# Chunk attention and a feed-forward layer on one core: V of the first two tiles by parity halves into one home, w_in's first half by pairs of K slices, and another order of the first loads and of the second tile's attention

## The chip, the cores and the metric

The kernel runs on one core of a Trainium2 chip. The metric is the device time of one execution in microseconds (us). TensorE is called PE, its weight load PEld, VectorE DVE, ScalarE ACT, GpSimd POOL, and SyncE, whose queue issues all DMAs here, SP.

## The reference

```python
# q, k, v: [8 batches, 8 heads, 576, 64], float32; chunks of 64 tokens
scores = q_c @ k_c.T / sqrt(64)            # within each chunk of 64 x 64
attn = softmax(scores); out = attn @ v_c
x = out.transpose(0, 2, 1, 3).reshape(4608, 512)
h = x @ w_in                               # 512 x 2048
g = 0.5 * h * (1 + erf(h / sqrt(2)))       # exact gelu
return g @ w_out                           # 2048 x 512, float32
```

## The kernel before

The 4608 tokens are cut into nine tiles of 512: tile t from 0 to 7 holds the first 512 tokens of batch t, and tile 8 the last chunk of every batch. For each tile the kernel computes attention, whose result `x` is kept transposed (model dimension on the partitions, four K slices of 128), then h = gelu(x @ w_in) in sixteen slots f of 128 hidden columns, then y = h @ w_out. All matmul operands are bf16; the inputs arrive as float32 in a pool of six 1 MB stage tiles (`arrival`) and are cast by DVE, ACT or POOL. Tile 0 multiplies densely; from tile 1 on seven products replace eight in both matrix products.

Everything is in program order on each engine (a manual schedule): where an instruction stands in the code sets when its engine gets to it. The attention of tiles 0 and 1 is cut into units per group g of two heads (G = 4): `T[2g]` and `T[2g+1]` transpose Q and K on PE (L207) and copy the results out of PSUM (Q by ACT at L213, K by ACT or DVE into the block-diagonal `k_bd` at L220), `S_[g]` is the scores (L366) and their exp on ACT (`pT`, L368), `att_sum` and `att_sums` the sums for the softmax (L374, L392), with reciprocals and transposes on DVE and `rb` copies on ACT (L403), and `A[g]` the product with V (L440) and its scaling into `x` on DVE (L442). The transposes of tile 1 share two PSUM banks (`ps_tp`), scores and outputs three (`ps_at`), h and y of tile 0 three (`ps_mm`).

V sits in `v_bd`, a block-diagonal home: head 2g fills rows 0 to 63 and columns 0 to 63 of a 128x128 block, head 2g+1 the other corner, and the other corners are zeros that a memset writes once. Tile 0 and tile 1 have a home each. V's loads bring 128 tokens on 128 partitions, so two chunks, and each head takes two casts (`cast_v`, L201), one for each chunk parity.

The order of tile 1's units between tile 0's y matmuls is written out as a table of hooks in `phase(0, {...})`: the number is a step of the second product. Steps 0 to 11 are slots f of h for all four row blocks (`mm2_rows`, L1025, four y matmuls each), steps 12 to 15 finish one row block each (`mm2_slot`, L989, four y matmuls). In slots 2 to 4 and in all of tile 0's h, `by_halves` (L465) splits each 512-column matmul in two. After the row blocks `rows_out` (L1004) copies y to `y_sb`, by ACT for the first three and by DVE for the last; the stores (L999), the DMA transposes of tile 2's Q and K (`flip`, L229) and V's rows (L152) follow on SP. Tile 1's h (L481, L491) comes next on PE, and tile 2's scores (L264) and V product (L349) within it and the second product of tile 1.

The loads at the start go out on SP in this order: Q and K of tile 0, V by head (L181), w_in in seven pieces (L1067), then w_out in four parts of 1 MB (L1075) with Q and K of tile 1 between them (L142), and V of tile 1.

Of the kernel before, what the change touches and what calls it, by code (L numbers as in the profile page):

```python
# [11 lines left out]
def kernel(  # L12
# [54 lines left out]
    NV = 2  # L67
    v_bds = [consts.tile([P, CT, G, P], bf16, name=f"v_bd{i}") for i in range(NV)]
    k_bds = [consts.tile([P, CT, P], bf16, name=f"k_bd{i}") for i in range(G)]

    def zero_v(i, eng):
        eng.memset(v_bds[i][0:CH, :, :, CH:P], 0.0)
        eng.memset(v_bds[i][CH:P, :, :, 0:CH], 0.0)

    def zero_k(k_bd, eng):
        eng.memset(k_bd[0:CH, :, CH:P], 0.0)
        eng.memset(k_bd[CH:P, :, 0:CH], 0.0)
# [120 lines left out]
    def cast_v(t, g, r, copies):  # L198
        to = slice(CH * r, CH * (r + 1))
        for c, copy in enumerate(copies):  # L200
            copy(v_bds[t % NV][to, c:CT:2, g, to], tiles[t]["vf"][CH * c:CH * (c + 1), 2 * g + r])  # L201

# [232 lines left out]
    def att_av(t, g):  # L435
        st = tiles[t]
        pool, tag = (ps_tp, "tp") if t == 1 and g > 1 else (ps_at, "at")
        av_ps = pool.tile([P, CT, CH], f32, tag=tag, name="av_ps")
        for i in range(CT):
            nc.tensor.matmul(av_ps[:, i, :], v_bds[t % NV][:, i, g, :], st["pT", g][:, i, :], start=True, stop=True)  # L440
        x, av, rc = st["x"][:, g, :], av_ps[:].rearrange("p i e -> p (i e)"), st["rc", g][:]
        nc.vector.tensor_tensor(x, av, rc.rearrange("p n e -> p (n e)"), op=mybir.AluOpType.mult)  # L442
# [17 lines left out]
    def by_halves(to, left, right, start, stop):  # L460

        n = to.shape[-1] // 2
        for a in range(2):
            cols = slice(n * a, n * (a + 1))
            nc.tensor.matmul(to[:, cols], left, right[:, cols], start=(start and a == 0), stop=stop, skip_group_check=True)  # L465

    def mm1_slices(t, pools, steps):

        st = tiles[t]
        st["h"] = hpool.tile([P, FF, MT], bf16, tag="h", name="h")  # L470
        h_ps = {}
        for step in steps:
            if callable(step):
                step()
                continue
            for ks in step[1]:
                for f in step[0]:
# [3 lines left out]
                    (nc.tensor.matmul if t else by_halves)(h_ps[f][:], w_in_sb[:, ks, f * P:(f + 1) * P], st["x"][:, ks, :],  # L481
                                                           start=(ks == 0), stop=(ks == KS - 1))
                    if ks == KS - 1:
                        nc.scalar.activation(st["h"][:, f, :], h_ps[f][:], Act.Gelu)

    def mm1_slot(t, f):
        if f == 0:
            tiles[t]["h"] = hpool.tile([P, FF, MT], bf16, tag="h", name="h")
        h_ps = ps_mm.tile([P, MT], f32, tag="mm", name="h_ps")
        for ks in range(KS):  # L490
            (nc.tensor.matmul if t else by_halves)(h_ps[:], w_in_sb[:, ks, f * P:(f + 1) * P], tiles[t]["x"][:, ks, :],  # L491
                                                   start=(ks == 0), stop=(ks == KS - 1))
        nc.scalar.activation(tiles[t]["h"][:, f, :], h_ps[:], Act.Gelu)  # L493
# [42 lines left out]
    def t_sum(i):  # L536
        v2 = v_bds[(i - 1) // 2][:].rearrange("p a b c -> p (a b c)")
        n = HF * HD
        return v2[:, (i - 1) % 2 * n:((i - 1) % 2 + 1) * n].rearrange("p (f n) -> p f n", f=HF)
# [472 lines left out]
    def mm2_rows(t, f):  # L1012

        last = MT // P - 1
        if f == 0:
            order = [(last, 0), (0, 0), (1, 0)]
        elif f == 1:
            order = [(last, 1), (0, 1), (1, 1), (2, 0), (2, 1)]
        else:
            order = [(ms, f) for ms in range(MT // P)]  # L1020
        for ms, fi in order:
            if fi == 0:
                pool, tag = (ps_at, "at") if ms == last else (ps_mm, "mm")
                tiles[t]["y_ps", ms] = pool.tile([P, d_model], f32, tag=tag, name="y_ps")
            (by_halves if 2 <= f < 5 else nc.tensor.matmul)(  # L1025
                tiles[t]["y_ps", ms][:], tiles[t]["h"][:, fi, ms * P:(ms + 1) * P], w_out_sb[:, fi, :],
                start=(fi == 0), stop=False)
# [35 lines left out]
    def load_w_in(c, parts=1):  # L1063
        raw = stage_tile()[:].rearrange("p (ks n) -> p ks n", ks=KS)
        n = WC // parts
        for a in range(parts):
            nc.sync.dma_start(raw[:, :, a * n:(a + 1) * n], w_in_v[:, :, c * WC + a * n:c * WC + (a + 1) * n])  # L1067
# [3 lines left out]
        return cast  # L1071
# [25 lines left out]
    with tc.manual_schedule():  # L1097
# [4 lines left out]
        win = [load_w_in(c, 2) for c in range(NWC - 1)]  # L1102
        act_table(Act.Exp)
# [6 lines left out]
        zero_k(k_bds[2], nc.gpsimd)  # L1110
        cast_qk(0, "k", 1, PO)
        zero_k(k_bds[3], nc.gpsimd)
        cast_qk(0, "k", 2, PO)
        cast_qk(0, "k", 3, PO)
        for g in range(G - 1):
            for r in range(2):
                cast_v(0, g, r, (PO, PO))
        cast_v(0, G - 1, 0, (PO, PO))
        win[0](0, PO)
# [29 lines left out]
        cast_v(0, G - 1, 1, (DV, DV))  # L1149
        A[2]()  # L1150
        win[0](1, AC)
        p3()
        A[3]()
        win.append(load_w_in(NWC - 1))
        wout = [load_w_out(0)]
        win[0](2, DV)
        win[0](3, PO)
        load_qk(1, "q")
        wout.append(load_w_out(1))
        for c in range(1, NWC):  # L1160
# [4 lines left out]
            if c == 1:  # L1165
                load_qk(1, "k")
            else:
                wout.append(load_w_out(c))
            if c < 3:
                r = slice(CH * (c - 1), CH * c)  # L1170
                o = slice(CH * (2 - c), CH * (3 - c))
                nc.gpsimd.memset(v_bds[1][r, :, :, o], 0.0)
# [9 lines left out]
        weight_sum(1)  # L1182
        for g in range(G):
            cast_qk(1, "k", g, DV if g % 2 == 0 else PO)
        for i in range(FC):
            wout[2](i, PO)
        for i in range(2):
            wout[3](i, PO)
        for g in (0, 2, 3):
            for r in range(2):  # L1190
                cast_v(1, g, r, (PO, PO))
# [7 lines left out]
        def sums():  # L1199
# [56 lines left out]
        for t in range(1, NT):  # L1256
# [8 lines left out]
            if t == 1:  # L1265
# [4 lines left out]
                for g in range(G):  # L1270
                    cast_qk(2, "k", g, DV)
# [96 lines left out]
```

## Time and profile before

| | us |
|---|---|
| median of 3 runs | 267.25 |
| lowest and highest | 266.49, 268.29 |
| the profiled execution's own time | 267.09 |
| its span in the profile | 265.5 |

| engine | busy us | share of the span |
|---|---|---|
| PE | 256.1 | 96% |
| DVE | 223.1 | 84% |
| ACT | 190.5 | 72% |
| POOL | 103.2 | 39% |

The span runs from the first to the last instruction of the one execution that the profiler recorded. Busy time is the time in which an engine had an instruction under way. A timeline row gives the start, the length, the engine and line, what is written and read, how many instructions it groups, and in brackets the idle time before it and what ended it. The mean granted clock of PE was 0.997.

### The profile page before, as it was taken

What the parts mean: (1) busy time and instruction counts of PE and PEld (TensorE: products, weight loads), DVE (VectorE), ACT (ScalarE), POOL (GpSimd) and SP (SyncE); (2) the same over time, 40 slices, a digit from 0 to 9 for tenths busy, and PEclk for the clock granted to TensorE, in tenths of its full rate; (3) what the DMA queues carried; (4) which work ended last, traced back from release to release, by engine and by line L of the source; (5) the groups of instructions that cost most, each with busy time, mean ns of one, the idle gap of its engine ahead of it and who ended that gap; (6) DMA issues with size and microseconds to landing.
All of it is one profiled execution on the core that took longest, in us unless ns stands there. A gap on an engine that the chain in (4) does not pass through costs nothing.

```text
span 265.5 us, 7854 instructions
## 1 busy us (share of the span) xinstructions
PE 256.1 (96%) x3122; PEld 210.6 (79%) x3122; DVE 223.1 (84%) x394; ACT 190.5 (72%) x386; POOL 103.2 (39%) x225
## 2 busy tenths in 40 slices
PE   6789999999999999999999999999999999999993
PEld 2478875556888888887888888888888888888882
DVE  6874986898897599678999999999999999948772
ACT  3856758987767987898888588947894789227720
POOL 7767778702364291481372095009411300000000
PEclk9999999999999999999999999999999999999998
DMA  6999998999979979999999988998973410130014
GB/s 201 268 311 396 395 401 236 283 193 289 243 195 284 220 175 244 275 239 249 276 245 232 267 186 237 217 175 195 264 160 80 134 42 2 41 119 3 2 40 125
DMA packets 123416, 54.02 MB, mean 203 GB/s; under 512 B 97776, under 2 KB 120304, under 8 KB 123376
## 3 DMA queue, kind: packets, MB, share of 16 engines
q1 hardware_dynamic: 123072, 53.23, 77.4%
q8 instruction: 25, 0.41, 0.7%
q10 hardware_dynamic: 304, 0.26, 0.3%
q14 instruction: 15, 0.12, 0.1%
HBM read 36.70 MB, written 9.44 MB: 174 GB/s over the span
## 4 chain that ended last, share of the span: by engine, by line
PE 76%; DMA 10%; ACT 7%; SPq 4%; issue 1%; DVE 0%; POOL 0%
PE hs_ps L601 31%; PE y_ps L761 22%; PE y_ps L791 13%; DMA arrival<-in_moe_w_out_dram 8%; ACT h L609 3%; SPq L181 2%; PE h_ps L491 2%; DMA arrival<-in_moe_w_in_dram 2%; PE av_ps L349 2%; PE h_ps L481 2%; ACT pT L272 2%; SPq L142 1%; PE y_ps L1025 1%; PE y_ps L989 1%; PE s_ps L264 1%; ACT L1095 1%
## 5 line engine op out<-in xcount | busy, mean ns | idle before, releaser
L609 ACT ACTIVATE h<-hs_ps 128x512 bf16<-128x512 f32 x87 | 49.6, 609 | 6.5 <-PE hs_ps L601 5.7
L238 POOL CAST v_nat<-arrival 128x256 bf16<-128x256 f32 x56 | 24.9, 473 | 33.5 <-DMA arrival<-in_v_dram 23.1
L601 PEld LDWEIGHTS <-w_in_sb 128*128 128x128 bf16 x348 | 33.9, 98 | 4.7 <-issue 0.2
L194 POOL CAST q_nat<-arrival 128x256 bf16<-128x256 f32 x40 | 16.8, 467 | 50.2 <-DMA arrival<-in_k_dram 25.3
L601 PE MATMUL hs_ps<-x,w_in_sb 128*128 128x256 bf16 x232 | 31.8, 272 | 0.0
L761 PEld LDWEIGHTS <-h 128*128 128x128 bf16 x240 | 23.2, 98 | 2.8
L1095 ACT ACT_TABLE_LOAD x16 | 20.5, 1283 | 1.3 <-PEq L1352 1.0
L190 POOL CAST k_nat<-arrival 128x256 bf16<-128x256 f32 (+1 forms) x44 | 19.1, 476 | 5.3 <-DMA arrival<-in_k_dram 5.3
L721 ACT COPY kept<-y_ps 128x512 f32<-128x512 f32 (+1 forms) x17 | 9.0, 536 | 16.0 <-PE y_ps L761 15.9
L761 PE MATMUL y_ps<-w_out_sb,h 128*128 128x256 bf16 x160 | 18.6, 273 | 0.0
L761 PE MATMUL y_ps<-v_bd,k_bd 128*128 128x256 bf16 x160 | 18.5, 273 | 0.1
L761 PEld LDWEIGHTS <-k_bd 128*128 128x128 bf16 x160 | 15.6, 98 | 2.1 <-issue 0.2
L618 ACT COPY hs_ps<-hs_ps 128x512 f32<-128x512 f32 x29 | 16.2, 583 | 0.6 <-PE hs_ps L601 0.5
L601 PE MATMUL hs_ps<-k_bd,w_in_sb 128*128 128x256 bf16 x116 | 16.6, 272 | 0.0
L493 ACT ACTIVATE h<-h_ps 128x512 bf16<-128x512 f32 x21 | 12.5, 604 | 5.5 <-PE h_ps L465 4.1
L272 ACT ACTIVATE pT<-s_ps 128x512 bf16<-128x512 f32 x28 | 14.4, 599 | 1.8 <-PE s_ps L264 1.8
L791 PEld LDWEIGHTS <-h 128*128 128x128 bf16 x144 | 13.8, 98 | 1.7
L465 PE MATMUL h_ps<-x,w_in_sb 128*128 128x256 bf16 x128 | 14.5, 273 | 0.1
L601 PE MATMUL hs_ps<-k_bd,w_in_more 128*128 128x256 bf16 x96 | 14.2, 273 | 0.0
L601 PEld LDWEIGHTS <-w_in_more 128*128 128x128 bf16 x128 | 12.5, 98 | 2.0 <-issue 0.3
L726 DVE TENSOR_TENSOR kept<-y_ps,kept 128x512 f32<-128x512 f32 (+1 forms) x16 | 10.4, 651 | 4.3 <-PE y_ps L761 2.3
L465 PEld LDWEIGHTS <-w_in_sb 128*128 128x128 bf16 x128 | 12.3, 98 | 2.1 <-DVE w_in_sb L1070 0.7
(175 smaller groups left out, 638.9 us busy)
## 6 DMA issues: line engine op xcount, KB each, us to landing
arrival<-in_v_dram SPq DMA_DIRECT2D x58, 128.0 KB, 3.2
arrival<-in_k_dram SPq DMA_DIRECT2D x28, 256.0 KB, 5.6
arrival<-in_q_dram SPq DMA_DIRECT2D x7, 1024.0 KB, 6.9
out_dram<-kept SPq DMA_DIRECT2D x24, 256.0 KB, 3.2
arrival<-in_moe_w_out_dram SPq DMA_DIRECT2D x4, 1024.0 KB, 12.1
arrival<-in_moe_w_in_dram SPq DMA_DIRECT2D x6, 512.0 KB, 8.5
out_dram<-y_sb SPq DMA_DIRECT2D x8, 256.0 KB, 2.5
arrival<-in_v_dram SPq DMA_DIRECT2D x28, 64.0 KB, 2.7
```

The costliest lines, as they stand in the source:

```text
L190: copy(st[nm][:, q0:q0 + n, g], st[nm + "f"][:, 2 * q0:2 * (q0 + n), g].rearrange("p (q r) d -> p q r d", r=2))
L194: copy(st[nm][:, g, j:j + 2].rearrange("p j r d -> p r j d"), st[nm + "f"][:, 2 * g:2 * g + 2, j:j + 2])
L238: copy(st["v"][:, r::2, n], st["vf"][:, r::2, n])
L272: nc.scalar.activation(pT[:].rearrange("p u (c j) -> p u c j", j=J), tiles[t]["s_ps"][m // 2][m % 2][:].rearrange("p u (j c) -> p u c j", ...
L465: nc.tensor.matmul(to[:, cols], left, right[:, cols], start=(start and a == 0), stop=stop, skip_group_check=True)
L493: nc.scalar.activation(tiles[t]["h"][:, f, :], h_ps[:], Act.Gelu)
L601: nc.tensor.matmul(hs[:, f], left[:, ks, f * P:(f + 1) * P], right[:, ks], start=(fresh and f == 0 and ks == 0), stop=(ks == 1), skip_grou ...
L609: nc.scalar.activation(h[:, n:n + HM, HD * c:HD * (c + 1)], src, Act.Gelu)
L618: "s11": lambda: AC(place_of("b")[:], bank["a"][:]),
L761: nc.tensor.matmul(to, left(f, m), right[:, f], start=(fresh and (split or m == 0) and f == 0), stop=(f == HF - 1), skip_group_check=True)
L791: nc.tensor.matmul(bank[name][:, m], left(f, m), right[:, f], start=(fresh and m == 0 and f == 0), stop=(f == HF - 1), skip_group_check=True)
L1095: nc.scalar.activation(act_scratch[:], rest[:, 0:1], func)
```

## The change

V of both tiles goes into `v_bds[0]`. `load_v` brings each head to 64 partitions, even heads to 0 to 63 and odd heads to 64 to 127, so that the eight chunks lie along the free dimension, and `cast_v` takes one instruction of 64x512 where it took two of 64x256. The second home's zeros are gone. Three of the four `k_bd` are zeroed by ACT copies from a tile of zeros (`rest`) instead of POOL memsets. w_in's first half of 512 KB is loaded and cast by pairs of K slices. w_out's parts are loaded in two halves each, Q and K of tile 1 as well, and w_out's third part comes ahead of K. `by_halves` is gone: tile 0's h and slots 2 to 4 of y use whole 512-column matmuls. The hooks of tile 1's units have other steps. Two of the four casts of tile 2's K go from DVE to POOL.

```diff
+    def by_copy(to):
+        nc.scalar.copy(to, rest[0:CH].rearrange("p (i c) -> p i c", c=CH))
...
-        tiles[t]["vf"] = stage_tile()[:].rearrange("p (h n d) -> p h n d", h=H, d=D)
+        tiles[t]["vf"] = stage_tile()[:].rearrange("p (g i d) -> p g i d", g=G, d=D)
         for h in range(H):
-            nc.sync.dma_start(tiles[t]["vf"][:, h], v[t, h, 0:MT, :].rearrange("(n key) d -> key n d", key=P))
+            r = h % 2
+            nc.sync.dma_start(tiles[t]["vf"][CH * r:CH * (r + 1), h // 2],
+                              v[t, h, 0:MT, :].rearrange("(i key) d -> key i d", key=CH))
...
-    def cast_v(t, g, r, copies):
-        to = slice(CH * r, CH * (r + 1))
-        for c, copy in enumerate(copies):
-            copy(v_bds[t % NV][to, c:CT:2, g, to], tiles[t]["vf"][CH * c:CH * (c + 1), 2 * g + r])
+    def cast_v(t, g, r, copy):
+        sl = slice(CH * r, CH * (r + 1))
+        copy(v_bds[0][sl, :, g, sl], tiles[t]["vf"][sl, g])
...
-                    (nc.tensor.matmul if t else by_halves)(h_ps[f][:], w_in_sb[:, ks, f * P:(f + 1) * P], st["x"][:, ks, :],
+                    nc.tensor.matmul(h_ps[f][:], w_in_sb[:, ks, f * P:(f + 1) * P], st["x"][:, ks, :],
...
-            (by_halves if 2 <= f < 5 else nc.tensor.matmul)(
+            nc.tensor.matmul(
...
-            nc.sync.dma_start(raw[:, :, a * n:(a + 1) * n], w_in_v[:, :, c * WC + a * n:c * WC + (a + 1) * n])
+            for k0 in range(0, KS, 2 if c + a == 0 else KS):
+                ks = slice(k0, k0 + 2 if c + a == 0 else KS)
+                nc.sync.dma_start(raw[:, ks, a * n:(a + 1) * n], w_in_v[:, ks, c * WC + a * n:c * WC + (a + 1) * n])
...
+        def cast_slices(k0, copy):
+            copy(w_in_sb[:, k0:k0 + 2, 0:n], raw[:, k0:k0 + 2, 0:n])
...
-        nc.sync.dma_start(raw, w_out_v[:, c * FC:(c + 1) * FC, :])
+        for f in range(0, FC, 2):
+            nc.sync.dma_start(raw[:, f:f + 2], w_out_v[:, c * FC + f:c * FC + f + 2, :])
...
-        zero_k(k_bds[0], nc.gpsimd)
-        zero_k(k_bds[1], nc.gpsimd)
-        zero_v(0, nc.vector)
+        zero_v(lambda to: nc.vector.memset(to, 0.0))
+        for g in range(G - 1):
+            zero_k(k_bds[g], by_copy)
+        zero_k(k_bds[G - 1], lambda to: nc.gpsimd.memset(to, 0.0))
...
-        win[0](0, PO)
+        first_slices(0, PO)
...
-        win[0](1, AC)
+        first_slices(2, DV)
         p3()
         A[3]()
...
-        win[0](2, DV)
+        win[0](2, AC)
         win[0](3, PO)
-        load_qk(1, "q")
+        load_halves("q")
...
-            if c == 1:
-                load_qk(1, "k")
+            if c == 2:
+                load_halves("k")
             else:
-                wout.append(load_w_out(c))
-            if c < 3:
-                r = slice(CH * (c - 1), CH * c)
-                o = slice(CH * (2 - c), CH * (3 - c))
-                nc.gpsimd.memset(v_bds[1][r, :, :, o], 0.0)
+                wout.append(load_w_out(2 if c == 1 else 3))
...
         phase(0, {0: [lambda: act_table(Act.Exp)],
-                      2: [T[0]], 3: [T[2]], 4: [T[4], T[6]], 7: [T[1], T[3]], 8: [T[5], S_[0]],
-                      9: [T[7], S_[1], next_qk], 10: [S_[2], lambda: att_sum(1, 0), lambda: wout[3](2, DV)],
-                      11: [lambda: wout[3](3, AC), S_[3]], 12: [lambda: cast_v(1, 1, 0, (AC, AC)), lambda: cast_v(1, 1, 1, (AC, AC)), sums],
-                      13: [A[0], lambda: over[0](2), lambda: over[0](3), U[1]], 14: [A[1], U[2]], 15: [A[2], U[3]]},
+                      4: [T[0], T[2], T[4]], 5: [T[6]], 9: [next_qk], 11: [T[1], T[3]],
+                      12: [T[5], T[7], S_[0], S_[1], S_[2], lambda: att_sum(1, 0), S_[3],
+                           lambda: cast_v(1, 1, 0, AC), lambda: cast_v(1, 1, 1, AC)],
+                      13: [sums], 14: [A[0], lambda: over[0](2), lambda: over[0](3), U[1]], 15: [A[1], U[2]],
+                      "end": [A[2], U[3]]},
               by_rows=True, first=2)
```

The first place is PE in tile 0's second product, from tile 1's first Q transpose on. `tp` is a transpose's PSUM tile, the first row of each group of matmuls is shown, and the weight loads between them are left out. Before:

```order
L207 MATMUL tp_658<-ident_60,q_nat_406 128x128
...
L465 MATMUL y_ps_648<-w_out_sb_86,h_484 128x256
...
L207 MATMUL tp_672<-ident_60,q_nat_406 128x128
...
L465 MATMUL y_ps_650<-w_out_sb_86,h_484 128x256
...
L207 MATMUL tp_686<-ident_60,q_nat_406 128x128
...
L207 MATMUL tp_692<-ident_60,q_nat_406 128x128
```

And of the change:

```order
L210 MATMUL tp_595<-ident_60,q_nat_400 128x128
...
L210 MATMUL tp_601<-ident_60,q_nat_400 128x128
...
L210 MATMUL tp_607<-ident_60,q_nat_400 128x128
...
L1021 MATMUL y_ps_577<-w_out_sb_86,h_477 128x512
...
L210 MATMUL tp_617<-ident_60,q_nat_400 128x128
```

The four transposes were spread over slots 2 to 4; now three stand together ahead of slot 4 and the fourth behind it.

The second place is PE further on, from tile 1's third K transpose to the sums. Before:

```order
L207 MATMUL tp_732<-ident_60,k_nat_460 128x128
...
L366 MATMUL s_ps_739<-s3_sb_87,k_bd0_81 128x64
...
L1025 MATMUL y_ps_648<-w_out_sb_86,h_484 128x512
...
L207 MATMUL tp_754<-ident_60,k_nat_460 128x128
...
L366 MATMUL s_ps_761<-s3_sb_87,k_bd1_82 128x64
...
L1025 MATMUL y_ps_650<-w_out_sb_86,h_484 128x512
...
L366 MATMUL s_ps_784<-s3_sb_87,k_bd2_83 128x64
...
L374 MATMUL sum_ps_795<-pT_748,ones_bd_65 128x512
...
L1025 MATMUL y_ps_655<-w_out_sb_86,h_484 128x512
...
L366 MATMUL s_ps_808<-s3_sb_87,k_bd3_84 128x64
...
L1025 MATMUL y_ps_646<-w_out_sb_86,h_484 128x512
...
L392 MATMUL sums_ps_827<-pT_748,ones_c_75 32x512
```

And of the change:

```order
L210 MATMUL tp_673<-ident_60,k_nat_461 128x128
...
L210 MATMUL tp_680<-ident_60,k_nat_461 128x128
...
L369 MATMUL s_ps_687<-s3_sb_87,k_bd0_81 128x64
...
L369 MATMUL s_ps_698<-s3_sb_87,k_bd1_82 128x64
...
L369 MATMUL s_ps_709<-s3_sb_87,k_bd2_83 128x64
...
L377 MATMUL sum_ps_720<-pT_696,ones_bd_65 128x512
...
L369 MATMUL s_ps_727<-s3_sb_87,k_bd3_84 128x64
...
L985 MATMUL y_ps_577<-w_out_sb_86,h_477 128x512
...
L395 MATMUL sums_ps_746<-pT_696,ones_c_75 32x512
```

The groups of four y matmuls between the K transposes and the scores went ahead of them, all of slots 0 to 11 now being done before the third K transpose; between the last scores and the sums stands one group, of the first row block.

The third place is SP, from w_in's last part to tile 1's V. Before:

```order
L1075 DMA arrival<-in_moe_w_out_dram 128x4x512
L142 DMA arrival<-in_q_dram 128x8x256
L1075 DMA arrival<-in_moe_w_out_dram 128x4x512
L142 DMA arrival<-in_k_dram 128x8x256
L1075 DMA arrival<-in_moe_w_out_dram 128x4x512 x2
L181 DMA arrival<-in_v_dram 128x4x64 x8
```

And of the change:

```order
L1077 DMA arrival<-in_moe_w_out_dram 128x2x512 x2
L144 DMA arrival<-in_q_dram 128x4x256 x2
L1077 DMA arrival<-in_moe_w_out_dram 128x2x512 x4
L144 DMA arrival<-in_k_dram 128x4x256 x2
L1077 DMA arrival<-in_moe_w_out_dram 128x2x512 x2
L184 DMA arrival<-in_v_dram 64x8x64 x8
```

K of tile 1 moved behind w_out's third part, every 1 MB load became two, and each head of V goes to 64 partitions.

More of the change, by code (lines that the diff above doesn't have):

```diff
@@ L65, with zero_v, zero_k @@
     nc.gpsimd.memset(ones_c[CH:P, QD // 2:QD], 1.0)
-    NV = 2
-    v_bds = [consts.tile([P, CT, G, P], bf16, name=f"v_bd{i}") for i in range(NV)]
+    v_bds = [consts.tile([P, CT, G, P], bf16, name=f"v_bd{i}") for i in range(2)]
     k_bds = [consts.tile([P, CT, P], bf16, name=f"k_bd{i}") for i in range(G)]
[L71 to L77, printed above, removed]
+    def zero_v(zero):
+        for r in range(2):
+            zero(v_bds[0][CH * r:CH * (r + 1), :, :, CH * (1 - r):CH * (2 - r)])
+    def zero_k(k_bd, zero):
+        for r in range(2):
+            zero(k_bd[CH * r:CH * (r + 1), :, CH * (1 - r):CH * (2 - r)])
+    def by_copy(to):
+        nc.scalar.copy(to, rest[0:CH].rearrange("p (i c) -> p i c", c=CH))
     NB = MT // 32
@@ L457, in att_units @@
         return T, S_, U, A
[L460 to L465, printed above, removed]
     def mm1_slices(t, pools, steps):
@@ L490, in mm1_slot @@
         for ks in range(KS):
-            (nc.tensor.matmul if t else by_halves)(h_ps[:], w_in_sb[:, ks, f * P:(f + 1) * P], tiles[t]["x"][:, ks, :],
+            nc.tensor.matmul(h_ps[:], w_in_sb[:, ks, f * P:(f + 1) * P], tiles[t]["x"][:, ks, :],
                                                    start=(ks == 0), stop=(ks == KS - 1))
@@ L1182 @@
         weight_sum(1)
+        for i in range(FC):
+            wout[2](i, PO if i % 2 == 0 else DV)
         for g in range(G):
@@ L1185 @@
         for i in range(FC):
-            wout[2](i, PO)
-        for i in range(2):
             wout[3](i, PO)
```

22 lines of the change are left out of this document (12 added, 10 removed).

## The prediction

> **What bounds the kernel now.** I read the page's busy shares first, then the table of windows, then the chain that ended last, then each engine's timeline between 9 and 60 us, which is the only stretch that the change touches.
>
> ```profile
> span 265.5 us, 7854 instructions
> PE 256.1 (96%) x3122; PEld 210.6 (79%) x3122; DVE 223.1 (84%) x394; ACT 190.5 (72%) x386; POOL 103.2 (39%) x225
> ```
>
> ```profile
> core 0: us, PE busy (x) PEld busy (x) DVE busy (x) ACT busy (x) POOL busy (x), PEclk, DMA share, GB/s
> 10.00:20.00 10.00, 8.22 (x121) 6.18 (x119) 7.89 (x16) 7.15 (x13) 7.32 (x17) 1.00 1.00 278
> 20.00:30.00 10.00, 9.86 (x89) 8.37 (x88) 6.34 (x9) 6.75 (x13) 8.21 (x8) 1.00 1.07 394
> 40.00:52.00 12.00, 11.68 (x117) 6.30 (x116) 9.41 (x16) 10.20 (x28) 8.96 (x20) 1.00 0.96 261
> 72.00:260.00 188.00, 187.91 (x2459) 165.26 (x2458) 165.48 (x295) 139.47 (x286) 58.13 (x136) 1.00 0.72 171
> ```
>
> From 72 us on PE misses 0.09 us of 188. So what the change gives or costs before then reaches the end of the span one for one, unless a later wait swallows it, and there is nothing left there to swallow. Between 10 and 30 us the DMA engines are full (share 1.00 and 1.07): there the loads set the pace. In 40 to 52 us PE still misses 0.3 us, with ACT busy 10.2 of 12.
>
> ```profile
> 18.78 22.29 DMA arrival<-in_moe_w_out_dram x2
> 41.13 0.62 POOL w_out_sb L1078
> 44.59 0.86 PE y_ps L1025 x4
> 52.01 3.67 PE h_ps L481 x17
> ```
>
> The chain that ended last runs over the w_out loads to 41.1 us and from there over PE alone; a group of four y matmuls is 0.86 us, so 0.215 each.
>
> **The start.** V's casts, the K zeros and the way to the first h matmuls:
>
> ```profile
> 5.81 1.17 ACT L220 COPY k_bd<-tp 64x512 bf16<-64x512 bf16 x2 [3.33 <-PE tp L207]
> 10.86 6.29 POOL L201 CAST v_bd<-arrival 64x256 bf16<-64x256 f32 x14
> 16.29 0.38 PE L440 MATMUL av_ps<-pT,v_bd 128*128 128x64 bf16 x7 [0.26 <-POOL v_bd L201]
> 17.95 14.30 PE L465 MATMUL h_ps<-x,w_in_sb 128*128 128x256 bf16 x125
> 21.17 0.43 DVE L1070 CAST w_in_sb<-arrival 128x512 bf16<-128x512 f32 x1 [1.74 <-DMA arrival<-in_moe_w_in_dram]
> 21.65 3.39 PEld L465 LDWEIGHTS <-w_in_sb 128*128 128x128 bf16 x32 [0.31 <-DVE w_in_sb L1070]
> 23.29 1.79 POOL L1172 MEMSET v_bd<- 64x2048 bf16 x1
> 25.42 6.67 PEld L465 LDWEIGHTS <-w_in_sb 128*128 128x128 bf16 x62 [0.38 <-DVE w_in_sb L1070]
> 17.29 0.61 POOL L1070 CAST w_in_sb<-arrival 128x512 bf16<-128x512 f32 x1
> ```
>
> Seven V casts of double size replace fourteen. A POOL cast of 128x512 is 0.61 us (last row), so they take 7 x 0.61 = 4.3 us instead of 6.29 and end near 15.2; PE's waits for V before h go, and h can begin some 0.6 us sooner. That is worth nothing: the fifth slot of h needs the next part of w_in, whose cast starts at 21.17 on the landing and lets PE go at 21.65. This gate stays, as the bytes ahead of it are the same. The six zero copies on ACT fill its idle 3.33 us; six at half of the 1.17 us in the first row are 3.5 us, so the first K copy is some 0.2 us late, before the same gate.
>
> Behind the gate there are twelve slots of four whole matmuls, 12 x 0.866 = 10.4 us, so y begins near 32.05. Before, it began at 32.42 by the row below: the 0.38 us stall at 25.42 (a DVE cast that ran slowly beside the POOL memset of 23.29, which is gone) and a few ns for each half matmul make the difference. **Term 1: -0.35 us**; bounds 0 (the stall returns as a landing wait) and -0.9 (the gate itself moves to 21.1, h being done by then).
>
> Whether V's loads keep their pace is the doubt here. V now goes to 64 partitions per transfer. V's stretch of the old load, in slices of 0.4 us from 4 us on, is the dip from slice 17 on (10.4 to 14 us, mean 202 GB/s):
>
> ```profile
> GB/s 323 305 220 264 317 364 328 325 348 361 358 344 302 294 263 270 165 187 222 169 197 223 243 180 235 307 282 297 274 320 305 323 348 300 310 305 358 420 351 374
> L139 SPq DMA_DIRECT2D arrival<-in_k_dram x8: 620/634/1213, 174.1 to 179.9; - x8
> ```
>
> So V's 1.05 MB takes 5.2 us now. The only 64-partition loads of that size in the trace (L139, 131 KB) are issued 5.8/7 = 0.83 us apart, 158 GB/s, which would make 6.6 us. Term 2 lies between 0 and +1.4 us of later landings; I take 0, because even and odd heads alternate between the two halves, the packets stay 256 bytes, and the L139 loads are paced by their issue (0.63 us, up to 1.21). The Trainium skill, SBUF — State Buffer, section "Door 1: The DMA port swizzle", speaks against the change: 64 partitions reach half of the ports, and it measured 196 GB/s for such a load of 1 MiB against 328 for 128 partitions. By its figure V would take 5.35 us, an estimate from that page, 0.15 us more, since the trace's 128-partition V never got the 328; so page and row differ on the old form and agree that the new one loses little.
>
> **The y phase.** Tile 1's transposes (T, L207), scores (S, L366), sums and attention outputs (A, L440) stand between tile 0's y matmuls:
>
> ```profile
> 32.42 1.89 PE L1025 MATMUL y_ps<-w_out_sb,h 128*128 128x512 bf16 x8
> 34.15 0.39 PE L207 MATMUL tp<-ident,q_nat 128*128 128x128 bf16 x4
> 34.64 0.57 ACT L213 COPY s_sb<-tp 128x512 bf16<-128x512 bf16 x1
> 39.81 1.17 ACT L220 COPY k_bd<-tp 64x512 bf16<-64x512 bf16 x2 [1.97 <-PE tp L207]
> 40.03 1.39 DVE L220 COPY k_bd<-tp 64x512 bf16<-64x512 bf16 x2 [0.29 <-PE tp L207]
> 41.03 0.38 PE L207 MATMUL tp<-ident,k_nat 128*128 128x128 bf16 x4 [0.17 <-ACT k_bd L220]
> 51.85 3.83 PE L481 MATMUL h_ps<-x,w_in_sb 128*128 128x512 bf16 x17
> ```
>
> A T costs PE 0.22 us (the rest of its 0.39 overlaps), its copy on ACT begins 0.49 us after it and takes 0.57 (Q) or 1.17 (K); on DVE K takes 1.39. The last row is the end of A3, at 51.85. The work between 32.42 and it is 64 y (13.76), 8 T (1.76), 4 S and 4 A at 0.23 (1.84), sum and sums (0.45), 3 h (0.65): 18.46 of 19.43, so old stalls were 0.97. The work stays the same; its new places need these waits, each behind the copies above, with two tp banks:
>
> - T4, third in a row: T0's copy ends 1.06 after T0 began, PE is there at 0.44. +0.65 with the hop.
> - T5 behind T1, T3 and four y: PE at 1.30, T1's copies done at 1.66. +0.36.
> - T7: T3's DVE copies end at 2.10, PE at 1.88. +0.22.
> - S2 needs T5's ACT copies, 3.32, PE at 2.78. +0.54.
> - sum needs the first exp (0.60), 3.92, PE at 3.55. +0.37.
> - sums, now only one y group behind S3, needs the fourth exp at about 5.7; PE at 5.25. +0.45.
>
> Together 2.6 us, and 0.15 for small hops. Nothing hides these: PE's queue is in order, and the y matmuls that used to stand between are now ahead of the burst (before: four y, 0.86 us, behind T5/S0, T7/S1 and S2 each). w_out's third part and K change places: at the 394 GB/s above a place of 1.05 MB is 2.7 us. K so comes near 41 us, the burst starts at about 43.1 (32.05 and the 44 y, 4 T and stall ahead of it), behind both. **Term 3: -0.97 + 2.75 = +1.8**; bounds +0.9 (ACT and DVE start sooner than 0.49) and +2.4 (the hops double).
>
> **What is late next.** ACT's order behind the burst:
>
> ```profile
> 42.65 1.26 ACT L368 ACTIVATE pT<-s_ps 128x512 bf16<-128x512 f32 x2
> 46.21 1.66 ACT L201 CAST v_bd<-arrival 64x256 bf16<-64x256 f32 x4
> 48.12 0.84 ACT L403 COPY rb<-early 32x16 f32<-32x16 f32 x4 [0.24 <-DVE early L397]
> 48.98 0.58 ACT L1004 COPY y_sb<-y_ps 128x512 f32<-128x512 f32 x1
> 49.59 1.70 ACT L403 COPY rb<-early 32x16 f32<-32x16 f32 x8
> 52.41 1.28 ACT L1095 ACT_TABLE_LOAD   x1
> 54.86 1.57 ACT L484 ACTIVATE h<-h_ps 128x512 bf16<-128x512 f32 x3 [0.95 <-PE h_ps L481]
> 53.30 0.68 DVE L1004 COPY y_sb<-y_ps 128x512 f32<-128x512 f32 x1
> 54.01 0.36 SPq L999 DMA_DIRECT2D out_dram<-y_sb  x1
> 59.74 2.19 SPq L229 DMA_TRANSPOSE k_t<-k_nat  x1
> 64.95 0.71 PE L264 MATMUL s_ps<-q_t,k_t 64*64 64x64 bf16 x64
> ```
>
> From T1 at 43.1 it now has 4 K copies (2.3), 4 exps (2.5), the V casts (1.3), 3 y_sb (1.7), 12 rb (2.5) and the table load (1.5) with no gap: ready for the first gelu near 55.6, which PE needs near 56.1. The old slack of 0.95 shrinks to some 0.5. The last x comes near 55.4, h needs it near 55.8. DVE's y_sb, behind that x, ends near 56.1 instead of 53.98, 2.1 late, while PE is 1.45 late. SP's store (54.01) waits for it, and behind the store queue the two flips, V's rows and the next loads. The K flip, issued until 61.93 before, is issued until 64.0, and the 64 score matmuls move from 64.95 to 66.4: 2.4 us are left for its transfer where there were 3.0. All this is covered, narrowly. Moving two K casts of tile 2 from DVE to POOL (idle then) costs nothing.
>
> **Sum.** -0.35 + 0 + 1.8 = +1.45. Against the profiled run's own 267.09 (span 265.5 and 1.6 around it; 0.16 under the median of 267.25) that gives **268.5 us**. With the bounds of the terms on their own: -0.9 + 0.9 = 0 to 0 + 2.4 = +2.4, so 267.1 to 269.5.
>
> **The rivals.** (A) ACT and SP lose their cover, slower. Place: ACT from the burst to the table load. Every 0.1 us beyond 0.5 that it slips goes into the first gelu, so into h's banks, and through the last x into the store and the K flip. It decides once the slip passes 0.5 us; a slip of 2.5 us (the gaps that ACT's quoted rows had, 1.97 ahead of the K copies and 0.24 ahead of rb, come back behind the later K, and 0.3 of waiting for y) adds 2.0: 270.5. For it: no idle left on ACT. Against: counted from measured durations, it just fits. (B) Faster: the waits are not there, as ACT and DVE serve the burst while PE runs y, and h's gate moves to 21.1: -0.9 from term 1, of term 3 the old 0.97 gone and 0.8 new: 267.09 - 1.07 = 266.0. Against: two banks and the order of PE's queue force T4, S2 and sum to wait. (C) V's 64-partition loads cost the 1.4 us of term 2; the queue is full, so every landing up to the gate is later: 268.5 + 1.4 = 269.9. Against: the alternating halves. (D) The change does not do what it says at all for the end: new stalls equal the old ones and the landing of K stays ahead: 267.1.
>
> **How the numbers follow.** Forecast 0.45, A 0.30, C 0.10, B 0.09, D 0.06. A bound of 1% of 267.25 (2.7 us: 264.6 and 269.9) is about what a measurement of this kernel tells from no change. Faster by over that only in a corner of B, 0.03. Slower: nearly all of A (0.27), half of C (0.05), a tail of the forecast (0.06): 0.38. The rest, 0.59, is within. The range reaches to B's better half below and past A above: 266.2 to 271.0; the forecast's own is 267.1 to 269.5.
>
> **What would show it.** Right: in the timeline of PE a wait of about 0.6 before the third Q transpose, waits of 0.2 to 0.5 behind ACT's k_bd copies, pT and before sums; y begins near 32.05; the 17 h matmuls begin near 53.3; waits from 72 us on unchanged. The gate near 21.6 still follows a w_in landing; if it comes at 23, C is right. A shows as PE waiting for the h banks near 57 or for k_t at the 64 score matmuls. Wrong altogether: the 17 h matmuls begin before 51.85, or a loss of over 0.5 us behind 72 us.

## The result and the profile after

The changed kernel takes 270.74 us (median of 5 runs, 269.11 to 271.21) against 267.25: its ratio to the kernel before, over all runs of both, is 1.012, with a 95% interval of 1.0075 to 1.0166. A second set of runs (e5 below) gave 1.0129 (1.0079 to 1.0178). It is slower by 1.2 to 1.3%, about 3.3 us. The forecast was 268.5; the measured time lies within the range of 266.2 to 271.0, and on the other side of the 1% line from the likeliest case. One execution of e8, 1.7% above that kernel's fastest, is left out of its ratio.

The page's first lines of the changed kernel's profiled execution (one of 271.21 us):

```profile
span 269.7 us, 7692 instructions
PE 257.0 (95%) x3046; PEld 203.5 (75%) x3046; DVE 220.6 (82%) x392; ACT 193.1 (72%) x389; POOL 99.0 (37%) x206
```

And its table of windows, with the columns of before:

```profile
core 0: us, PE busy (x) PEld busy (x) DVE busy (x) ACT busy (x) POOL busy (x), PEclk, DMA share, GB/s
10.00:20.00 10.00, 8.00 (x112) 5.01 (x110) 8.34 (x16) 6.52 (x11) 5.40 (x9) 1.00 0.89 235
20.00:30.00 10.00, 9.03 (x42) 4.00 (x42) 3.97 (x9) 6.97 (x12) 5.48 (x7) 1.00 1.07 395
40.00:52.00 12.00, 11.20 (x101) 5.82 (x100) 8.46 (x15) 6.67 (x14) 8.85 (x14) 1.00 0.76 213
72.00:260.00 188.00, 186.68 (x2445) 163.75 (x2442) 165.14 (x292) 140.34 (x290) 60.95 (x138) 1.00 0.78 176
```

PE is busy about as long as before (257.0 against 256.1 us) and idles more, above all in three places: 0.83 us more in 20 to 30 us, 0.48 more in 40 to 52, and 1.23 more behind 72. Between 10 and 20 us the DMA share fell from 1.00 to 0.89 and the rate from 278 to 235 GB/s.

The start, from the timelines of ACT, POOL and PE (start, length, what, and in brackets the idle time before it):

```profile
2.39 3.75 ACT L79 COPY k_bd<-rest 64x512 bf16<-64x512 bf16 x6
11.83 4.64 POOL L204 CAST v_bd<-arrival 64x512 bf16<-64x512 f32 x7
20.50 0.62 ACT L1068 CAST w_in_sb<-arrival 128x512 bf16<-128x512 f32 x1 [2.03 <-DMA arrival<-in_moe_w_in_dram]
18.01 2.19 PE L477 MATMUL h_ps<-x,w_in_sb 128*128 128x512 bf16 x8
21.18 12.26 PE L487 MATMUL h_ps<-x,w_in_sb 128*128 128x512 bf16 x56 [0.97 <-ACT w_in_sb L1068]
```

The DMA rate in slices of 0.4 us from 4 us on:

```profile
GB/s 259 246 305 259 371 294 312 302 302 338 315 361 324 291 251 231 190 144 106 259 130 238 204 206 191 211 296 319 251 207 259 218 246 238 271 266 256 282 300 356
```

h starts as before (18.01, then 17.95): V's seven casts are as short as forecast (4.64 us), but they begin at 11.83 where they began at 10.86, as V's first load lands at 11.5 and not at 10.7. PE now waits at the third slot, 0.97 us, for the second 512 KB of w_in, which hold the weights of h's third and fourth slots and land at 20.5. (The texts call w_in's first 512 KB, for the first two slots, its first half, and these its second quarter; w_in has 4 MB in all.) Before, that part was in SBUF in time and the gate was the fifth slot, at 21.65. From the new gate fourteen slots are left instead of twelve, so y begins at 33.27, not at 32.42. In the DMA row the rate behind V, from 14.4 to 18.8 us, is 207 to 319 GB/s, where the old row has 274 to 358.

The y phase, from PE's timeline, the waits in brackets:

```profile
33.27 3.62 PE L1021 MATMUL y_ps<-w_out_sb,h 128*128 128x512 bf16 x16
37.79 0.38 PE L210 MATMUL tp<-ident,q_nat 128*128 128x128 bf16 x4 [0.45 <-ACT s_sb L216]
45.92 0.38 PE L210 MATMUL tp<-ident,k_nat 128*128 128x128 bf16 x4 [0.17 <-ACT k_bd L223]
46.46 0.38 PE L210 MATMUL tp<-ident,k_nat 128*128 128x128 bf16 x4 [0.15 <-POOL w_out_sb L1080]
47.57 0.41 PE L369 MATMUL s_ps<-s_sb,k_bd 128*128 128x64 bf16 x8 [0.26 <-ACT k_bd L223]
48.19 0.38 PE L377 MATMUL sum_ps<-pT,ones_bd 128*128 128x512 bf16 x1 [0.21 <-ACT pT L371]
54.25 3.83 PE L477 MATMUL h_ps<-x,w_in_sb 128*128 128x512 bf16 x17
```

These are the waits that were forecast, one behind the other, but for the one before the sums; a bracket holds the idle time after the earlier matmul's modelled end, so it is some 0.17 us less than what the queue loses. The wait at 46.46 is put down to a cast on POOL that ended last before it, at 46.38; the bank that the transpose needs came free with DVE's copies of T3, at 46.31:

```profile
44.92 1.39 DVE L223 COPY k_bd<-tp 64x512 bf16<-64x512 bf16 x2 [1.13 <-PE tp L210]
```

From the first y to the end of A3 it takes 54.25 - 33.27 = 20.98 us instead of 51.85 - 32.42 = 19.43: 1.55 more. A3 ends 2.40 us later.

What was to be covered behind the burst, and a wait late in the span, from the timelines of ACT, DVE, SP and PE:

```profile
57.26 2.56 ACT L480 ACTIVATE h<-h_ps 128x512 bf16<-128x512 f32 x5 [0.58 <-PE h_ps L477]
56.56 0.68 DVE L1000 COPY y_sb<-y_ps 128x512 f32<-128x512 f32 x1
57.27 0.36 SPq L995 DMA_DIRECT2D out_dram<-y_sb  x1
67.55 0.71 PE L267 MATMUL s_ps<-q_t,k_t 64*64 64x64 bf16 x64
133.12 0.71 PE L267 MATMUL s_ps<-q_t,k_t 64*64 64x64 bf16 x64 [1.17 <-DMA k_t<-k_nat]
```

ACT still idles 0.58 us before the first gelu (it was 0.95), and tile 2's scores at 67.55 do not wait. Tile 5's scores do, 1.17 us, for a K that its DMA transpose brought late. That is nearly all of what this execution lost behind 72 us. Its time is 4.1 us above the profiled run of before: 2.4 by A3's end, 1.2 here, 0.5 in small pieces.

### The profile page after: what moved, and what is told of

Its sections match the earlier page's. It is cut to its first block, busy times and chain, and to the rows that moved or that the text cites. A ratio compares the mean times of both kernels' runs of the same rounds, so it can differ in the third digit from the quotient of the medians.

```text
span 269.7 us, 7692 instructions
## 1 busy us (share of the span) xinstructions
PE 257.0 (95%) x3046; PEld 203.5 (75%) x3046; DVE 220.6 (82%) x392; ACT 193.1 (72%) x389; POOL 99.0 (37%) x206
## 4 chain that ended last, share of the span: by engine, by line
PE 59%; DMA 12%; SPq 11%; POOL 8%; DVE 5%; ACT 2%; issue 2%; DVEq 0%; POOLq 0%
PE hs_ps L597 23%; PE y_ps L757 18%; DMA arrival<-in_q_dram 6%; PE y_ps L787 6%; PE h_ps L487 5%; PE y_ps L1021 4%; POOL v_nat L241 4%; SPq L184 3%; SPq L138 3%; DMA arrival<-in_moe_w_in_dram 2%; SPq L232 2%; POOL q_nat L198 2%; POOL k_nat L194 2%; DMA k_t<-k_nat 2%; SPq L144 2%
## 5 line engine op out<-in xcount | busy, mean ns | idle before, releaser
L597 PEld LDWEIGHTS <-w_in_sb 128*128 128x128 bf16 x348 | 33.9, 98 | 4.8 <-issue 0.2
L241 POOL CAST v_nat<-arrival 128x256 bf16<-128x256 f32 x56 | 27.4, 526 | 26.8 <-DMA arrival<-in_v_dram 17.0
L194 POOL CAST k_nat<-arrival 128x256 bf16<-128x256 f32 (+1 forms) x46 | 20.7, 494 | 5.4 <-DMA arrival<-in_k_dram 5.3
L1097 ACT ACT_TABLE_LOAD x16 | 20.5, 1283 | 1.3 <-PEq L1354 1.0
L487 PE MATMUL h_ps<-x,w_in_sb 128*128 128x512 bf16 x84 | 19.1, 379 | 1.0 <-ACT w_in_sb L1068 1.0
L757 PE MATMUL y_ps<-v_bd,k_bd 128*128 128x256 bf16 x160 | 18.5, 273 | 0.1
L275 ACT ACTIVATE pT<-s_ps 128x512 bf16<-128x512 f32 x28 | 14.4, 598 | 3.1 <-PE s_ps L267 3.0
L487 PEld LDWEIGHTS <-w_in_sb 128*128 128x128 bf16 x84 | 8.1, 97 | 10.3 <-ACT w_in_sb L1068 1.5
```

What stands on the lines that cost most here:

```text
L194: copy(st[nm][:, q0:q0 + n, g], st[nm + "f"][:, 2 * q0:2 * (q0 + n), g].rearrange("p (q r) d -> p q r d", r=2))
L241: copy(st["v"][:, r::2, n], st["vf"][:, r::2, n])
L275: nc.scalar.activation(pT[:].rearrange("p u (c j) -> p u c j", j=J), tiles[t]["s_ps"][m // 2][m % 2][:].rearrange("p u (j c) -> p u c j", ...
L487: nc.tensor.matmul(h_ps[:], w_in_sb[:, ks, f * P:(f + 1) * P], tiles[t]["x"][:, ks, :], start=(ks == 0), stop=(ks == KS - 1))
L597: nc.tensor.matmul(hs[:, f], left[:, ks, f * P:(f + 1) * P], right[:, ks], start=(fresh and f == 0 and ks == 0), stop=(ks == 1), skip_grou ...
L757: nc.tensor.matmul(to, left(f, m), right[:, f], start=(fresh and (split or m == 0) and f == 0), stop=(f == HF - 1), skip_group_check=True)
```

## The experiments

All ratios are to the kernel before in the same set of runs, with their 95% intervals. Besides the time, two numbers are read from each profile, so from a single execution: when y begins, and how long it takes from there to the end of A3 (the y phase).

| kernel | ratio (95%) | y begins | y to A3's end |
|---|---|---|---|
| before (first profile) | 1 | 32.42 | 19.4 |
| changed kernel (first profile) | 1.0120 (1.0075 to 1.0166) | 33.27 | 21.0 |
| e5: changed kernel again | 1.0129 (1.0079 to 1.0178) | 33.83 | 21.0 |
| e1: changed, V on 128 partitions | 1.0103 (1.0065 to 1.0142) | 32.45 | 21.4 |
| e2: changed, old table | 1.0106 (1.0072 to 1.0139) | 32.60 | 21.4 |
| e9: changed, w_in's first half as before | 1.0078 (1.0045 to 1.0110) | 31.38 | 21.0 |
| e10: as e9, and V on 128 partitions | 1.0087 (1.0048 to 1.0127) | 31.24 | 21.4 |
| e7: changed, old order and table | 1.0100 (1.0061 to 1.0138) | 33.47 | 19.1 |
| e11: as e7, and w_in's first half as before | 1.0029 (0.9993 to 1.0065) | 32.80 | 19.7 |
| e3: before, new table | 1.0085 (1.0053 to 1.0117) | 31.20 | 22.7 |
| e4: before, V on 64 partitions | 1.0020 (0.9998 to 1.0043) | 31.92 | 19.9 |
| e12: before, w_in by pairs of slices | 0.9996 (0.9970 to 1.0022) | 32.06 | 19.2 |
| e8: before, whole matmuls | 1.0007 (0.9986 to 1.0028) | 32.70 | 19.3 |
| e6: changed, half of V of tiles 3 and 4 | 1.0152 (1.0115 to 1.0189) | 35.48 | 21.0 |

The first four runs ask which of two parts costs: V's loads at the start, or the burst of tile 1's units.

**e1, V back on 128 partitions in the changed kernel.**

```diff
-        tiles[t]["vf"] = stage_tile()[:].rearrange("p (g i d) -> p g i d", g=G, d=D)
+        tiles[t]["vf"] = stage_tile()[:].rearrange("p (h n d) -> p h n d", h=H, d=D)
...
-        copy(v_bds[0][sl, :, g, sl], tiles[t]["vf"][sl, g])
+        for c in range(2):
+            copy(v_bds[0][to, c:CT:2, g, to], tiles[t]["vf"][CH * c:CH * (c + 1), 2 * g + r])
```

> The changed kernel with V loaded to 128 partitions as before (each head two casts again), all else as changed. Theory 1 (the 64-partition V loads make w_in land late): w_in's second quarter lands near 18.5 to 19.3 instead of 20.5 us, h's wait of 0.97 shrinks or moves to the next part of w_in near 21.6, y begins near 32.2 instead of 33.3, and the time falls by 0.9 to 1.2 (more if the wait for tile 4's K flip at 131 us goes too): 268.4 to 269.8. Theory 2 (only the burst of tile 1's units costs): y's start moves by under 0.3 us, time within 0.4 of the changed kernel's 270.7.

The timelines of ACT and PE:

```profile
19.16 0.62 ACT L1067 CAST w_in_sb<-arrival 128x512 bf16<-128x512 f32 x1 [0.88 <-DMA arrival<-in_moe_w_in_dram]
22.08 10.53 PE L486 MATMUL h_ps<-x,w_in_sb 128*128 128x512 bf16 x48 [0.34 <-DVE w_in_sb L1067]
```

The second quarter lands at 19.2, the gate is back at the fifth slot, and y begins at 32.45: the start behaves as the first theory says. By ratio the time fell by some 0.5 us (1.0120 to 1.0103), less than the 0.9 to 1.2 that it said, and its interval overlaps the changed kernel's, so by time alone this run decides nothing. The y phase is 0.4 us longer than the changed kernel's, 21.4, as it is in e10, which has V's double casts too.

**e2, the old table in the changed kernel** (the steps of the diff's removed lines, without the two w_out casts).

> The changed kernel with the table of steps for tile 1's units of before. Theory 2: from the first y to the end of A3 it takes 19.4 to 19.7 us instead of 21.0, the time falls by 1.3 to 1.6: 269.2, and to 268 if the wait for tile 4's K flip goes too. Theory 1 alone: y still begins near 33.3, and the time falls by under 0.5. Theory 3 (K of tile 1 comes later, so the old table no longer fits): waits of 1 us or more before the K transposes of slot 7, time not below 270.

PE's timeline at the first K transposes:

```profile
41.54 0.87 PE L210 MATMUL tp<-ident,k_nat 128*128 128x128 bf16 x8 [1.84 <-DVE k_nat L200]
```

The third theory's wait is there: with K behind w_out's third part, the old table asks for K 1.84 us before it has been cast, and the span from y to A3's end is 21.4. (The median, 269.84, is a little under the 270 that the theory gave.) The table and the order of the loads belong together: with the new order, the old table is not measurably better than the new one.

**e3, the new table in the kernel before.**

> The kernel before with the changed table alone (w_out's last part cast wholly by POOL as in the change). Theory 2: the span from the first y to A3's end grows from 19.4 to 21.0, time +1.5: 268.8. If the burst is only costly together with the later K and w_out: growth under 0.7, 267.3 to 267.9.

PE's timeline, from the first y to the end of A3:

```profile
31.20 1.89 PE L1025 MATMUL y_ps<-w_out_sb,h 128*128 128x512 bf16 x8
35.73 0.38 PE L207 MATMUL tp<-ident,q_nat 128*128 128x128 bf16 x4 [0.45 <-ACT s_sb L213]
40.91 2.75 PE L1025 MATMUL y_ps<-w_out_sb,h 128*128 128x512 bf16 x12 [1.11 <-POOL w_out_sb L1078]
46.79 0.41 PE L366 MATMUL s_ps<-s_sb,k_bd 128*128 128x64 bf16 x8 [0.33 <-ACT k_bd L220]
53.87 2.32 PE L481 MATMUL h_ps<-x,w_in_sb 128*128 128x512 bf16 x10
```

1.0085, or 2.3 us: the table alone makes this kernel slower. But not all of it is the burst: the 22.7 us hold the burst and 1.3 us at 40.9 for w_out's third part, still behind K here, a wait that the changed kernel's order avoids; without it the span is 21.4. This execution began y at 31.20, the kernel before in its profile at 32.42 with the same code up to there, so starts differ by 1.2 us between executions, and a difference of that size between two profiles shows nothing by itself.

**e4, V on 64 partitions in the kernel before** (loads and single casts as in the change).

> The kernel before with V's loads to 64 partitions and one cast for each head, both homes kept. Theory 1: w_in's parts land 1 to 1.5 us later, the slot of h that waits for w_in does so until 22.5 or later, y begins 0.8 to 1.2 us later, time +0.8 to +1.2: 268.2. Rival (the cast halves win what the landings lose): 266.9 to 267.4.

The timelines of DVE (the cast of w_in's third load) and PE:

```profile
20.63 0.43 DVE L1071 CAST w_in_sb<-arrival 128x512 bf16<-128x512 f32 x1 [1.33 <-DMA arrival<-in_moe_w_in_dram]
31.92 1.89 PE L1026 MATMUL y_ps<-w_out_sb,h 128*128 128x512 bf16 x8
```

In this execution y does not begin later, so the start does not bear the first theory out. The time decides less: alone V's form costs 0 to 0.4%, or 0 to 1.1 us, and the theory asked for 0.8 to 1.2.

The second set asks whether the wait for tile 5's K makes the difference, and what is left without burst and order.

**e5, the changed kernel again**, as the control.

> The changed kernel once more, as the control of this set. From the profiles so far: +2.2 to +2.4 us from tile 1's burst and the loads around it in every execution, and in some executions 1 to 2 us more where tile 5's scores wait for their K transposed by DMA (131 us). So times in two groups, 2.3 and 3.5 to 4.5 above the kernel before of this set, ratio 1.009 to 1.015. If the late wait were in all of them or in none, one group.

PE's timeline at h's third slot:

```profile
21.73 12.26 PE L487 MATMUL h_ps<-x,w_in_sb 128*128 128x512 bf16 x55 [1.69 <-ACT w_in_sb L1068]
```

The runs took 268.44 to 272.35, spread out rather than in two groups. In this profile nothing waits for tile 5's K; h waits 1.69 us at its third slot.

**e6, less to load ahead of tile 5's flips.** The odd heads' V of tiles 3 and 4 is not loaded.

```diff
-        rows_128(t, tiles[t]["vf"], parity)
+        rows_128(t, tiles[t]["vf"], (0,) if t in (3, 4) else parity)
```

> The changed kernel without the odd heads' V loads of tiles 3 and 4 (their casts read the even heads again, so part of the computation is left out): 1 MB less on SP's queue ahead of tile 5's flips. Theory (late wait by the queue's lateness): tile 5's K is in place over 3 us before its scores, no wait there, no group at +3.5 to +4.5: +2.2 to +2.4 us over the kernel before, ratio 1.0085. Rival (the wait is not from the queue's lateness but from the flip itself, or the slow executions are slow elsewhere): the same times as the control.

PE's timeline at h's third slot and at tile 5's scores:

```profile
21.69 13.95 PE L488 MATMUL h_ps<-x,w_in_sb 128*128 128x512 bf16 x55 [2.39 <-ACT w_in_sb L1069]
133.88 0.71 PE L268 MATMUL s_ps<-q_t,k_t 64*64 64x64 bf16 x64
```

And its table of windows:

```profile
core 0: us, PE busy (x) PEld busy (x) DVE busy (x) ACT busy (x) POOL busy (x), PEclk, DMA share, GB/s
22.00:27.00 5.00, 5.00 (x17) 1.96 (x16) 1.71 (x4) 2.42 (x5) 3.15 (x4) 0.68 1.06 380
```

No wait at tile 5's scores, and no gain: 1.0152. So that wait, real as it is in two profiles (1.17 us in the first, 1.96 in e2), is not needed for a long execution. This one, the longest of its six, lost its time at the start, in two ways: 2.39 us at the third slot, and h behind it took 13.95 us instead of 12.26, as PE's granted clock was 0.68 from 22 to 27 us (0.992 over the span). Of y's late begin at 35.48 some 1.7 us are therefore the clock and not a load. The rival held.

**e7, the old order of loads, casts and table in the changed kernel.**

> The changed kernel with K of tile 1 ahead of w_out's third part again (loads and casts) and with the table of before; all else as changed (V by halves of partitions and single casts, w_in by pairs of K slices, zeros by ACT, whole matmuls, loads in halves). Theory (burst and order together are the cost): the first y to A3's end takes 19.4 to 19.9 us, time within 0.5 of before, at best 0.5 below: ratio 0.998 to 1.002. Rival (the V and w_in loads cost too): y starts 0.5 to 1 us later and that stays: ratio 1.003 to 1.005.

PE's timeline at h's third slot, the first y and the end of A3:

```profile
21.37 12.26 PE L487 MATMUL h_ps<-x,w_in_sb 128*128 128x512 bf16 x55 [1.26 <-ACT w_in_sb L1068]
33.47 1.89 PE L1021 MATMUL y_ps<-w_out_sb,h 128*128 128x512 bf16 x8
52.56 3.62 PE L477 MATMUL h_ps<-x,w_in_sb 128*128 128x512 bf16 x16
```

The y phase is short again, 19.1, but the time is still 1.0% up, more than either theory gave: a second cost is there, and the profile has it at h's third slot. Up to that place V, w_in, the zeros and the whole matmuls differ.

**e8, whole matmuls in the kernel before.**

> The kernel before with whole 512-column matmuls in place of the halves in tile 0, nothing else. From 152 fewer matmul pieces at about 3 ns: between -0.4 and 0 us, ratio 0.9985 to 1.000. Where the loads set the pace of that stretch, 1.000. If the halves hid something (a wait that now shows), above 1.002.

1.0007 (0.9986 to 1.0028): no difference that this could tell. (The pieces saved are 76, by the pages' counts of 3122 and 3046 instructions on PE in the first two profiles, not 152.)

The last set separates that second cost. The theory was then that the pair slices of w_in and V on 64 partitions do it together.

**e9, w_in's first half in one piece** in the changed kernel.

```diff
-            for k0 in range(0, KS, 2 if c + a == 0 else KS):
-                ks = slice(k0, k0 + 2 if c + a == 0 else KS)
-                nc.sync.dma_start(raw[:, ks, a * n:(a + 1) * n], w_in_v[:, ks, c * WC + a * n:c * WC + (a + 1) * n])
+            nc.sync.dma_start(raw[:, :, a * n:(a + 1) * n], w_in_v[:, :, c * WC + a * n:c * WC + (a + 1) * n])
...
-        first_slices(2, DV)
+        win[0](1, AC)
```

> The changed kernel with w_in's first half loaded in one piece and cast as before; V stays on 64 partitions. Theory 4 (the pair slices and V on 64 partitions together make w_in's second quarter land at 20.5 to 21 instead of 18.5 us, so that h waits 1.0 to 2.6 us): it lands by 18.7 again, h's wait sits at the next part and is under 0.5, y begins by 32.5, time 0.8 to 1.2 below the changed kernel: ratio to before 1.003 to 1.008. Rival (V on 64 partitions alone makes it late, the kernel before only had luck in its start): landing 19.5 or later, ratio within 0.002 of the changed kernel's 1.013.

The timelines of PE and DVE:

```profile
19.20 12.34 PE L487 MATMUL h_ps<-x,w_in_sb 128*128 128x512 bf16 x56
20.52 0.43 DVE L1066 CAST w_in_sb<-arrival 128x512 bf16<-128x512 f32 x1 [1.54 <-DMA arrival<-in_moe_w_in_dram]
31.38 3.62 PE L1021 MATMUL y_ps<-w_out_sb,h 128*128 128x512 bf16 x16
52.35 3.83 PE L477 MATMUL h_ps<-x,w_in_sb 128*128 128x512 bf16 x17
```

The wait is gone, y begins 1.9 us earlier than in the changed kernel's first profile, and the ratio falls to 1.0078, as theory 4 said, though its interval still overlaps the changed kernel's. The row at 20.52 shows why the wait is gone. It is the third w_in load, and it lands when the third one lands in the changed kernel, 20.5. But there the third load is the second quarter, for h's third slot, since the first half takes two; here it is the next part, for the fifth slot, and PE asks for it near 21.

**e10, w_in's first half in one piece and V on 128 partitions.**

> As the last, and V on 128 partitions with two casts as well; left of the change are tile 1's table and order of loads, the zeros by ACT, the whole matmuls and the halves of loads. Theory 4: start as before (y by 32.5), the y phase 21 to 21.4, so the burst's cost alone: ratio 1.006 to 1.0085, and under the one with V on 64 partitions by no more than 0.002.

1.0087: not to be told from e9. With w_in whole, V's form makes no difference to the time that shows here either; the y phase is 0.4 us longer, 21.4, as it is in e3 without its w_out wait.

**e11, old order, table and w_in.**

> The changed kernel with the order of loads, the table and w_in's first half of before; left are V on 64 partitions with single casts, the zeros by ACT, the whole matmuls and the loads in halves. Theory 4: neither cost is left: y by 32.5, y phase 19.0 to 19.5, ratio 0.999 to 1.003. Rival (V or the zeros or the halves of loads cost by themselves): 1.005 or more.

1.0029 (0.9993 to 1.0065): both costs are taken out, and what is left, V's form, the zeros, the whole matmuls and the loads in halves together, can't be told from nothing. Its profile is a little behind what was expected: y begins at 32.80 and the y phase is 19.7.

**e12, the pair slices alone in the kernel before.**

> The kernel before with w_in's first half by pairs of K slices (loads and casts as in the change) alone. Theory 4 with an interplay of both: w_in's second quarter lands near 19 and h's wait stays under 0.6, ratio 0.999 to 1.002. If the slices alone do it: it lands at 20 or later, h waits over 1 us at its third slot, y begins near 33.3, ratio 1.003 to 1.006.

The timelines of ACT (the cast of the third load) and PE:

```profile
18.54 0.62 ACT L1072 CAST w_in_sb<-arrival 128x512 bf16<-128x512 f32 x1 [0.55 <-DMA arrival<-in_moe_w_in_dram]
32.06 1.89 PE L1025 MATMUL y_ps<-w_out_sb,h 128*128 128x512 bf16 x8
```

Alone they cost nothing that shows (0.9970 to 1.0022): here, with V on 128 partitions, the third load lands at 18.5, before h's third slot needs it. No run here beat the kernel before; e12 and e8 equal it.

## Why the prediction was right in its range, and where it was wrong

**What bounds the kernel: right in the main.** What the stretch before 60 us loses reaches the end of the span. But one wait behind 72 us, at tile 5's K, was over the 0.5 us that the prediction had named as a sign of being wrong altogether.

**Term 3, the burst: right.** Forecast +1.8 (0.9 to 2.4); measured +1.55 in the first profile, and 21.0 to 21.4 us for the y phase in every kernel that has the new table and no wait for a load in it, against 19.1 to 19.9 with the old one. Its waits stand at the third Q transpose, the third and fourth K transposes, the third scores and the sum. The one that hardly came is the wait before the sums: they begin at 49.59, as ACT's four exps end, at 49.60.

**Terms 1 and 2, the start: the step that failed.** The prediction put h's gate at the fifth slot, "as the bytes ahead of it are the same", and took 0 for later landings. What counted was the place in the queue, not the bytes: PE waits for a part, and the split of the first half moved the second quarter from the second load to the third in the queue behind V. That load lands at 20.5, and the gate came at the third slot, 21.18. So the start measured +0.85 (33.27 against 32.42) where -0.35 was forecast, 1.2 us off. One profile could mislead here, but all five profiles with the slices and V on 64 partitions wait at the third slot, 0.97 to 2.39 us, and begin y at 33.27, 33.83, 35.48 (1.7 of it by the clock), 33.47 and, e2, 32.60; the nine others begin it between 31.20 and 32.80. Together with the 1.55 of the y phase that is the 2.40 by which A3 is late, against the 1.45 forecast.

**What each is worth in time.** Four kernels that else are alike make a table of two by two: e11 1.0029 with neither, e9 1.0078 with the new order and table, e7 1.0100 with the slices, and the changed kernel 1.0120 and 1.0129 with both. So the slices cost 0.7 and 0.5%, the new order and table 0.5 and 0.2%, each difference uncertain by about 0.5%. Averaged, an estimate from the intervals, that is 0.6% (1.5 us) for the slices and 0.4% (1.0 us) for order and table, each known to about 0.35%. So the term that was put at nothing costs no less than the burst that was forecast, and the latter is only just clear of the noise in these pairs; its waits in the profiles and e3 show it too.

**Rival C** named the place and nearly the size (every landing 1.4 us later, 269.9) but not the mechanism: V on 64 partitions costs nothing by itself that e4 could tell (0 to 0.4%), nor do the slices (e12). With both, the third load is late and also needed early. That the slices matter is shown (e9, e11); V's share is not: e1, which takes V out, is not measurably faster, and in two profiles with V on 128 partitions the third load was just as late, where nothing needed it early. The estimate by the Trainium skill, SBUF — State Buffer, "Door 1: The DMA port swizzle", was 0.15 us for V; e4's 0 to 0.4% of the time fits it and does not test it.

**Rival A** was wrong in its first part: ACT kept 0.58 us of cover and tile 2's K came in time. The loss of cover on SP did come, but at tile 5's K and in two profiles only; e5, e6 and e7 are slower than the kernel before without it.

**The chances.** Slower by over 1% had 0.38, mostly through A. It came true by the sum of the forecast's own burst and C's start. That the time fell within the range was in part luck: the range reached that high to make room for A, which did not happen, and the forecast's own bounds, 267.1 to 269.5, left out the 1.4 us that the prediction itself had given term 2.

What stays open: why the third w_in load lands so unevenly. With V on 64 partitions it was between 19.8 and 21.9 in eight profiles, with V on 128 partitions 18.5 to 19.2 in four, but 21.2 in the kernel before and 21.5 in e8. So V's form is not all of it, and the time of that landing varies from execution to execution: 20.5 and 21.1 in the changed kernel and e5, the same program. SP's records bear on it: V's eight loads kept it busy for 7.1 to 8.3 us on 64 partitions and for 6.1 to 7.4 on 128, so that w_in's first load went out at 12.2 to 13.4 instead of 11.2 to 12.6 us. No run here separates that from the landing itself. Nor is the 0.7% between e7 and e11 in the profiles, whose A3 ends stand at 52.6 and 52.5; the profiled execution of e7 (268.50) is one of its faster ones, that of e11 (268.22) is above its median of 267.76.

## What to carry to other kernels

Before a load is split, look which place in the queue each part gets, and which instruction waits for that part; here a split moved everything behind it back by a place though no byte was added. Count a burst of dependent units on an in-order engine by the copies between them: the matmuls that stood between transposes, scores and sums were the cover, and moving them ahead cost 1.55 us of the y phase. Where edits look harmless alone, try them together: the slices measured nothing in the kernel before, and about 0.6% with V on 64 partitions.

## What the runs showed of the hardware that was not expected

The same code up to y began it at 31.20 (e3) and at 32.42 (before): w_in's first load landed at 16.3 and 17.2 us and its third at 19.0 and 21.1. And fewer bytes ahead did not bring a load sooner: with V on 64 partitions the third w_in load landed at 20.5 us with 1.0 MB of w_in up to its end (the changed kernel) and with 1.5 MB (e9), and the next three at 21.92, 23.26 and 24.58 against 21.90, 23.25 and 24.59.
